# Three units' lone scores beside their state additions, one scan behind q's products, later output parts ahead of masks

## The chip, the cores and the metric

The kernel runs on one core of one Trainium2 chip. The metric is the device time of one launch in microseconds, as the median of several runs. Times in rows count from the start of the profiled span. TensorE does the matmuls, VectorE, ScalarE and GpSimd the elementwise work, SyncE issues the DMA loads and stores.

## The reference

A gated linear attention with a state of 48 x 48 for each of 8 heads and 4 sequences of 768 tokens, and behind it a gated layer of 384 to 1536 to 384 features over all 3072 tokens.

```
state = alpha[:, :, t, :, None] * state + einsum('bhd,bhe->bhde', k[:, :, t], v[:, :, t])
y[:, :, t] = einsum('bhd,bhde->bhe', q[:, :, t], state)
...
gate = 1.0 / (1.0 + exp(-(x @ w_gate)))
val = x @ w_val
out = gate * val @ w_out        # x is y with the heads side by side, [3072, 384]
```

## The kernel before

The 3072 tokens are cut into 6 groups of 512. The attention of a group is done for 4 pairs of heads, one pair at a time: a unit is one pair in one group, so there are 24 units, u = 4 g + p. Units 0 to 5 work on chunks of 128 tokens (`unit`), units 6 to 23 on chunks of 64 (`late`). The gated layer of a group takes 12 steps, one for each 128 of the 1536 hidden features; step s has f = s % 12 and group s // 12. The attention of a group runs during the steps of the group before it.

A step (`step`, L734) is two products of nine matmuls of 128x512 each (gate and value, L317: three chunks of x, by high and low parts), the sigmoid on ScalarE (L752), the gating product on VectorE (L754, in place in the PSUM bank of the value), its high part on ScalarE (hh, L756) and the remainder on VectorE (hl, L757, which reads the same bank), and the output part: six matmuls with hh and three with hl (L765), a step later. The products of a step and the outputs of units share three PSUM banks in turn, pg, pv and at2.

A late unit loads its rows of decay and k into `in0` or `in1` (L634, alternately), q into A (L640), v (L642) and a second copy of v (L645). VectorE scans the decays twice (G, L480, from `in`; F, L484), with small operations between (L482, L486, L483); GpSimd multiplies k by G in place in `in` (L488); VectorE multiplies q by F (A, two halves, L650) and transposes k (kn, 16 pieces, L663). TensorE computes the scores (L672, 16 matmuls into at0 and at1, from A and `in`), the additions to the state (L679, from kn and v, other columns of at0 and at1) and, for the unit before, the outputs (L715). VectorE then updates the state (L698, 8 operations) and multiplies the scores by a mask (L685, 4 operations); GpSimd makes vs from the state (L703). The output is split into high part (yt, L524 on ScalarE) and remainder (yt, L525 on VectorE), and two or six transfers (L532) turn it into x, of which the products of the next group read. The load into `in0` or `in1` must wait for the scores, the transposes and GpSimd of the unit that used it last.

All this is recorded as 1500 odd parts, each with an engine, a time and a key (`Plan.add`). `Plan.order` works out a due time for each part from its key and its users, and a list schedule by these ranks. Then a table of pairs, `MOVES`, is applied in order: (n, m) takes part n out of its engine's queue and puts it right behind part m. Each engine works through its own queue in that order; between engines semaphores hold. The keys of a unit are set in `begin`: o is the step at whose end the unit's output is due, y = o - 3; the state updates have y + 0.55, the masks y + 0.6, the outputs o + 0.52. The parts of `finish` (both yt and the transfers) have the key t["y"], which is None, so that only their users' due times rank them.

Of the kernel before, what the change touches and what calls it, by code (L numbers as in the profile page):

```python
# [19 lines left out]
B, H, S, D = 4, 8, 768, 48  # L20
# [36 lines left out]
def in_turns(t):  # L57
# [56 lines left out]
)  # L114


# [204 lines left out]
def chunked(ctx, tc, rows, vc, vh, weights_in, out, const, ident, flags, weights, within):  # L321
# [65 lines left out]
    mask = {n: sb.tile([P, n], F32, name=f"mask{n}") for n in (C, E)}  # L387
# [149 lines left out]
    def unit(u, g, p, t):  # L537
# [33 lines left out]
        plan.add("tensor", (0.25 * nch + 0.1, 0.5), t["A"], scores, [(inn, "k"), (inn, "q")], [x[0] for x in pas])  # L571
        plan.add("tensor", (0.09 * nch + 0.1, 0.5), t["Y"], adds, [*((knn, a) for a in range(4)), (vn, "v")], [pkn])

# [56 lines left out]
    def late(u, g, p, t):  # L630
# [50 lines left out]

        plan.add("tensor", (0.045 * EH, 0.5), t["Y"], adds, [*((knn, a) for a in range(4)), (vn, "v")], [x[0] for x in pas], fixed=True)
        for j, (pan, pa) in enumerate(pas):
# [110 lines left out]
    def begin(u):  # L794
        g, p = divmod(u, NP)
        if u < EARLY:
            t = dict.fromkeys(("load", "G", "dec", "kt", "q", "X", "kn", "Y", "A", "mask", "S", "sd", "out", "y"))
            t.update(flag=14.0 + u, run=1, e_k="vector" if u in (0,) else "gpsimd", e_q="vector" if u in (0,) else "gpsimd")
        else:
            o = last_step(u)  # L800
            y = o - 3
            t = dict(load=y - 5, G=y - 2.9, dec=y - 2, kt=y - 2.7, flag=y + 1 + 0.5 * p, q=y - 2.0, X=y - 0.50, A=y + 0.50, kn=y - 1,
                     Y=y + 0.51, mask=y + 0.6, S=y + 0.55, sd=y + 0.7, out=o + 0.52, y=None)
        return unit(u, g, p, t) if u < EARLY else late(u, g, p, t)

    def last_step(u):

        return NF * (u // NP - 1) + 10 - 3 * (NP - 1 - u % NP)

    for u in range(NP):  # L810
        for _ in begin(u):
            pass
    for f in range(NF):
        weight_piece(f, None)
    now = begin(NP)
    next(now), next(now)
    finished = {last_step(u): u for u in range(NP, NG * NP)}
    for s in range(NG * NF):
        step(s)
        if s in finished:  # L820
            u = finished[s]
            following = begin(u + 1) if u + 1 < NG * NP else iter((None, None))
            next(following)
            next(now, None)
            next(following)
            now = following
# [12 lines left out]
        out=within, in0=total[1][0:1, 0:1], scalar1=G_BOUND, scalar2=None, op0=ALU.is_le), [total[0]])  # L839
# [127 lines left out]
```

## Time and profile before

| | |
|---|---|
| three runs, us | 518.01, 518.13, 518.69; median 518.13 |
| the profiled execution, us | 518.39, span 516.6, mean granted TensorE clock 0.998 |
| TensorE (PE) | 506.4 us, 98% of the span, 4114 matmuls |
| VectorE (DVE) | 397.4 us, 77% |
| ScalarE (ACT), GpSimd (POOL) | 164.0 us, 32%; 88.6 us, 17% |
| DMA | 55.69 MB, mean 108 GB/s |

A timeline row is: start in us, length in us, engine, line, operation, what it writes <- what it reads, count, and in brackets the engine's idle time before it and what ended it. Rows that follow each other on one engine with the same line and tiles are merged. Lengths of matmuls overlap, since ends are modelled; starts are what counts. Group 2 begins with the product that starts at 196.32, group 3 at 276.89, group 4 at 357.47.

### The profile page before, as it was taken

Reading aid. Unit: us, or ns where it says so; the run is one execution under the profiler, and the core shown is the slowest. Engines: PE = TensorE matmul, PEld = TensorE weight load, DVE = VectorE, ACT = ScalarE, POOL = GpSimd, SP = SyncE. Lnnn points to the kernel's source line nnn. Section 1 sums busy time; section 2 is a strip of 40 time slices with the busy share of each in tenths; the row PEclk is TensorE's granted clock in tenths of the full one; section 3 lists DMA queues with packets and bytes.
Section 4 is the critical chain, followed back from the end, with each engine's and each line's share of the span. In section 5 each row is a group of like instructions: output and inputs, shape, how many; then the busy total and the mean of one; then the engine's idle time right before and its main releaser. Section 6 shows DMA issues by size and latency. Waiting matters only on the chain.

```text
span 516.6 us, 10389 instructions
## 1 busy us (share of the span) xinstructions
PE 506.4 (98%) x4114; PEld 422.1 (82%) x4114; DVE 397.4 (77%) x866; ACT 164.0 (32%) x304; POOL 88.6 (17%) x129
## 2 busy tenths in 40 slices
PE   7999999999999999999999999999999999999995
PEld 4688888888888888888888888887888888888884
DVE  8999999998989999979889969799978532222221
ACT  2566666624112222212222321222322212311211
POOL 4632131103121122211121201211401000000000
PEclk9999999999999999999999999999999999999999
DMA  8757796840633433421423423404522011100001
GB/s 318 289 180 233 245 282 184 242 96 32 186 81 87 121 101 130 86 93 36 128 76 93 136 41 98 115 16 126 155 34 72 3 34 36 61 1 0 1 0 65
DMA packets 23093, 55.69 MB, mean 108 GB/s; under 512 B 3712, under 2 KB 10880, under 8 KB 23040
## 3 DMA queue, kind: packets, MB, share of 16 engines
q1 hardware_dynamic: 22752, 54.58, 35.8%
q8 instruction: 34, 0.56, 0.5%
q10 hardware_dynamic: 288, 0.39, 0.2%
q14 instruction: 19, 0.16, 0.1%
HBM read 41.39 MB, written 4.72 MB: 89 GB/s over the span
## 4 chain that ended last, share of the span: by engine, by line
PE 88%; DVE 7%; DMA 2%; issue 1%; POOL 1%; ACT 0%; SPq 0%; DVEq 0%
PE po L765 26%; PE pv L317 19%; PE pg L317 18%; PE at L317 15%; PE at L672 2%; PE pg L715 1%; PE at L679 1%; DMA A<-in_rows_dram 1%; PE pv L715 1%; DVE G L480 1%; DMA x<-yt 1%; DVE kn L663 1%; PE at L715 1%; DVE F L484 1%; PE at L500 1%
## 5 line engine op out<-in xcount | busy, mean ns | idle before, releaser
L765 PE MATMUL po<-hh,w 128*128 128x512 f32 x432 | 112.8, 387 | 0.0
L317 PE MATMUL pv<-x,w 128*128 128x512 f32 x468 | 111.9, 382 | 0.0
L317 PE MATMUL pg<-x,w 128*128 128x512 f32 x459 | 109.7, 382 | 0.0
L317 PEld LDWEIGHTS pv<-x,w 128*128 128x128 f32 x468 | 87.6, 188 | 15.3
L317 PEld LDWEIGHTS pg<-x,w 128*128 128x128 f32 x459 | 85.9, 188 | 15.0 <-ACT w L452 0.2
L765 PEld LDWEIGHTS po<-hh,w 128*128 128x128 f32 x432 | 79.6, 188 | 14.2
L317 PE MATMUL at<-x,w 128*128 128x512 f32 x369 | 88.2, 382 | 0.8 <-DMA x<-yt 0.8
L317 PEld LDWEIGHTS at<-x,w 128*128 128x128 f32 x369 | 69.0, 188 | 13.1 <-issue 1.2
L663 DVE STREAM_TRANSPOSE kn<-in 32x128 f32<-32x128 f32 x224 | 67.8, 303 | 4.6 <-PE at L679 0.8
L765 PE MATMUL po<-hl,w 128*128 128x512 f32 x216 | 62.9, 383 | 0.0
L703 POOL TENSOR_TENSOR vs<-st,dec 64x384 f32<-64x384 f32 x36 | 30.6, 850 | 154.4 <-DVE st L698 153.1
L488 POOL TENSOR_TENSOR in<-in,G 128x512 f32<-128x512 f32 x21 | 28.1, 1337 | 144.2 <-DVE G L480 57.8
L765 PEld LDWEIGHTS po<-hl,w 128*128 128x128 f32 x216 | 40.4, 188 | 7.4 <-DVE hl L757 0.2
L698 DVE SCALAR_TENSOR_TENSOR st<-st,dec,at 128x48 f32<-128x48 f32 x144 | 38.0, 264 | 7.4 <-PE at L679 1.5
L754 DVE TENSOR_TENSOR pv<-pv,sg 128x512 f32<-128x512 f32 x31 | 21.2, 685 | 24.5 <-PE pv L317 22.9
L754 DVE TENSOR_TENSOR at<-at,sg 128x512 f32<-128x512 f32 x21 | 14.4, 685 | 28.6 <-PE at L317 28.6
L756 ACT CAST hh<-pv 128x512 fp32r<-128x512 f32 x31 | 18.2, 587 | 54.8 <-DVE pv L754 50.9
L752 ACT ACTIVATE sg<-pg 128x512 f32<-128x512 f32 x31 | 18.5, 597 | 47.2 <-PE pg L317 47.2
L754 DVE TENSOR_TENSOR pg<-pg,sg 128x512 f32<-128x512 f32 x20 | 13.7, 686 | 24.1 <-PE pg L317 24.0
L685 DVE TENSOR_TENSOR A<-at,mask 64x256 f32<-64x256 f32 x72 | 30.4, 422 | 1.3
L650 DVE TENSOR_TENSOR A<-A,F 64x512 f32<-64x512 f32 x36 | 25.8, 717 | 3.4 <-DMA A<-in_rows_dram 2.6
L756 ACT CAST hh<-at 128x512 fp32r<-128x512 f32 x21 | 12.3, 586 | 50.7 <-DVE at L754 50.7
(163 smaller groups left out, 511.2 us busy)
## 6 DMA issues: line engine op xcount, KB each, us to landing
in<-in_rows_dram SPq DMA_DIRECT2D x18, 516.5 KB, 3.9
raw<-in_w_dram SPq DMA_DIRECT2D x12, 575.8 KB, 4.8
x<-yt SPq DMA_DIRECT2D x30, 216.0 KB, 3.6
first_w<-in_w_dram SPq DMA_DIRECT2D x10, 575.8 KB, 5.0
A<-in_rows_dram SPq DMA_DIRECT2D x36, 128.0 KB, 3.8
v<-in_vc_dram SPq DMA_DIRECT2D x22, 192.0 KB, 4.7
vs<-in_vh_dram SPq DMA_DIRECT2D x36, 96.0 KB, 3.6
out_dram<-raw SPq DMA_DIRECT2D x10, 256.0 KB, 2.2
```

What stands on the lines that cost most here:

```text
L317: nc.tensor.matmul(out=dst, lhsT=lhs(a, i), rhs=rhs(b, i), start=(n == 0 and i == 0), stop=(n == len(todo) - 1 and i == NK - 1))
L488: plan.add(e, vec(n) if e == "vector" else pool_(n), t["kt"], lambda: getattr(nc, e).tensor_tensor(out=kT, in0=kT, in1=G, op=ALU.mult), [g ...
L650: plan.add("vector", vec(T), t["q"], lambda j=j: nc.vector.tensor_tensor(out=A[own[j], j], in0=A[own[j], j], in1=F[own[j]], op=ALU.mult), ...
L663: nc.vector.transpose(out=kn[32 * b:32 * b + 32, :, 32 * a:32 * a + 32], in_=blocks[32 * a:32 * a + 32, b])
L685: plan.add("vector", 0.42, t["mask"], lambda pa=pa, j=j, i=i: nc.vector.tensor_tensor(out=A[other[j], j].rearrange("p (c i t) -> p i c t", ...
L698: nc.vector.scalar_tensor_tensor(out=st[:, c + 1, :], in0=st[:, c, :], scalar=dec[:, c:c + 1], in1=pas[c % 2][1][:, T // 2 + c // 2 * D:T ...
L703: plan.add("gpsimd", pool_(EH * D), t["sd"], lambda j=j: nc.gpsimd.tensor_tensor(out=vs[own[j], j], in0=st[own[j], 0:EH], in1=dec[own[j]]. ...
L715: nc.tensor.matmul(out=py[R * j:R * j + D, cs], lhsT=vs[r, j, c, :], rhs=A[r, j, cs], start=True, stop=True)
L752: plan.add("scalar", act(T), None, lambda: nc.scalar.activation(out=sg, in_=got["g"][1][:, 0:T], func=AF.Sigmoid), [got["g"][0]], [sgn], s ...
L754: plan.add("vector", vec(T), None, lambda: nc.vector.tensor_tensor(out=pv, in0=pv, in1=sg, op=ALU.mult), [sgn], [pvn], soon=soon)
L756: plan.add("scalar", act(T), None, lambda: nc.scalar.copy(out=stored(hh), in_=quarters(pv)), [pvn], [hhn], soon=soon)
L765: nc.tensor.matmul(out=pso_now[m][1][:, 0:T], lhsT=weights.part("o", b, f)[:, m * P:(m + 1) * P], rhs=in_turns(h[a]), start=(f == 0 and i ...
```

## The change

```
@@ MOVES
     (664, 608), (778, 664), (663, 778), (851, 661), (736, 848), (735, 736), (606, 781), (779, 782),
+    (854, 790), (945, 914), (1239, 1208), (1539, 1508),
 )
@@ begin
             t = dict(load=y - 5, G=y - 2.9, dec=y - 2, kt=y - 2.7, flag=y + 1 + 0.5 * p, q=y - 2.0, X=y - 0.50, A=y + 0.50, kn=y - 1,
-                     Y=y + 0.51, mask=y + 0.6, S=y + 0.55, sd=y + 0.7, out=o + 0.52, y=None)
+                     Y=y + 0.51, mask=y + 0.6, S=y + 0.55, sd=y + 0.7, out=o + 0.52, y=o + 0.54 if u >= 12 else None)
```

Part 854 is the scan G of unit 8, part 790 the second half of unit 7's A*F: the scan, which stood directly ahead of the two halves in VectorE's queue, stands directly behind them. Parts 945, 1239 and 1539 are the scores of units 9, 13 and 17, parts 914, 1208 and 1508 the second products of the second steps of groups 2, 3 and 4. The new key gives the yt parts and the transfers of units 12 to 23 a rank just ahead of the next unit's state updates and masks. The added line in `MOVES` makes every line number below it one higher in the changed kernel.

TensorE's queue at the start of group 2 (w0 and w1 are the weights of its first two steps, x0 its tokens, w10 and w11 the last of group 1), before, and then changed; of the 16 rows of scores and the 8 of additions the first stand:

```order
L765 MATMUL po2_130<-hl0_121,w10_1081 128x512
L672 MATMUL at0_123<-A1_91,in1_80 64x64
...
L317 MATMUL pg0_126<-x0_115,w0_346 128x512 x9
L317 MATMUL pv0_127<-x0_115,w0_346 128x512 x9
...
L317 MATMUL at2_125<-x0_115,w1_461 128x512 x9
L317 MATMUL pg0_126<-x0_115,w1_461 128x512 x9
L679 MATMUL at0_123<-v1_82,kn0_88 48x48 x2
```

```order
L766 MATMUL po2_130<-hl0_121,w10_1081 128x512
L318 MATMUL pg0_126<-x0_115,w0_346 128x512 x9
L318 MATMUL pv0_127<-x0_115,w0_346 128x512 x9
...
L318 MATMUL at2_125<-x0_115,w1_461 128x512 x9
L318 MATMUL pg0_126<-x0_115,w1_461 128x512 x9
L673 MATMUL at0_123<-A1_91,in1_80 64x64
...
L680 MATMUL at0_123<-v1_82,kn0_88 48x48 x2
```

The scores of unit 9, which read in1, move behind two steps' products and stand directly ahead of the additions; groups 3 and 4 begin in the same way.

VectorE's queue at the same place, from the remainder of step 24 on (G1 with in1 and dec3 is unit 11, st1 unit 9), before, and then changed; of the 8 rows of state updates and the 4 of masks the first stand:

```order
L757 TENSOR_TENSOR hl0_121<-pv0_127,hh0_119 128x4x128
L782 COPY raw0_83<-po1_129 128x512
L480 SCALAR_TENSOR_TENSOR G1_95<-in1_80,d1g64_106 128x512
...
L754 TENSOR_TENSOR pg0_126<-pg0_126,sg0_117 128x512
L698 SCALAR_TENSOR_TENSOR st1_112<-st1_112,dec1_101,at0_123 128x48
...
L757 TENSOR_TENSOR hl1_122<-pg0_126,hh1_120 128x4x128
L685 TENSOR_TENSOR A1_91<-at0_123,mask64_108 64x4x64
...
L525 TENSOR_TENSOR yt0_89<-pv0_127,yt0_89 128x4x128
```

```order
L758 TENSOR_TENSOR hl0_121<-pv0_127,hh0_119 128x4x128
L783 COPY raw0_83<-po1_129 128x512
L481 SCALAR_TENSOR_TENSOR G1_95<-in1_80,d1g64_106 128x512
...
L755 TENSOR_TENSOR pg0_126<-pg0_126,sg0_117 128x512
L699 SCALAR_TENSOR_TENSOR st1_112<-st1_112,dec1_101,at0_123 128x48
...
L758 TENSOR_TENSOR hl1_122<-pg0_126,hh1_120 128x4x128
L526 TENSOR_TENSOR yt0_89<-pv0_127,yt0_89 128x4x128
L686 TENSOR_TENSOR A1_91<-at0_123,mask64_108 64x4x64
```

Only yt moves, ahead of the four masks; the scan G1 stays ahead of the gating product, the state updates and hl1. SyncE's queue is unchanged here, with the load of in1 ahead of the stores of group 1.

VectorE's queue at the start of group 3 (G1 with dec3 is now unit 15), before, and then changed:

```order
L480 SCALAR_TENSOR_TENSOR G0_94<-in0_79,d1g64_106 128x512
...
L757 TENSOR_TENSOR hl0_121<-at2_125,hh0_119 128x4x128
L782 COPY raw0_83<-po1_129 128x512
L480 SCALAR_TENSOR_TENSOR G1_95<-in1_80,d1g64_106 128x512
...
L663 STREAM_TRANSPOSE kn0_88<-in0_79 32x4x32 x8
L484 SCALAR_TENSOR_TENSOR F1_97<-in1_80,d1f_104 128x512
```

```order
L481 SCALAR_TENSOR_TENSOR G0_94<-in0_79,d1g64_106 128x512
...
L783 COPY raw0_83<-po1_129 128x512
L758 TENSOR_TENSOR hl0_121<-at2_125,hh0_119 128x4x128
...
L664 STREAM_TRANSPOSE kn0_88<-in0_79 32x4x32 x8
L481 SCALAR_TENSOR_TENSOR G1_95<-in1_80,d1g64_106 128x512
...
L485 SCALAR_TENSOR_TENSOR F1_97<-in1_80,d1f_104 128x512
```

The scan G1 moves behind the transposes of unit 14, to the place of its F1, and the load of in1 moves behind the stores of group 2 on SyncE; the start of group 4 is rearranged in the same way. On GpSimd the product of k follows its scan.

## Rows read from the trace of the kernel before

**Rows 1.** The page's first part: busy us (share of the span) x instructions.

```profile
PE 506.4 (98%) x4114; PEld 422.1 (82%) x4114; DVE 397.4 (77%) x866; ACT 164.0 (32%) x304; POOL 88.6 (17%) x129
```

**Rows 2.** Timeline of TensorE, a joined block in group 2 and what follows it.

```profile
226.00 0.69 PE L672 MATMUL at<-A,in 48*64 48x64 f32 x32
...
228.01 1.60 PE L765 MATMUL po<-hh,w 128*128 128x512 f32 x6
```

**Rows 3.** Timeline of TensorE, start of group 2: around lone scores, then additions and outputs.

```profile
194.94 0.83 PE L765 MATMUL po<-hl,w 128*128 128x512 f32 x3
...
196.32 2.26 PE L317 MATMUL pg<-x,w 128*128 128x512 f32 x9
198.41 2.14 PE L317 MATMUL pv<-x,w 128*128 128x512 f32 x9
...
206.43 0.57 PE L679 MATMUL at<-v,kn 64*48 64x48 f32 x32
...
207.97 1.60 PE L765 MATMUL po<-hh,w 128*128 128x512 f32 x6
209.40 0.82 PE L765 MATMUL po<-hl,w 128*128 128x512 f32 x3
210.06 2.14 PE L317 MATMUL at<-x,w 128*128 128x512 f32 x9
212.04 2.14 PE L317 MATMUL pg<-x,w 128*128 128x512 f32 x9
```

**Rows 4.** Timeline of VectorE and of TensorE near 165, and a later pair A*F.

```profile
161.74 1.23 DVE L480 TENSOR_TENSOR_SCAN G<-in,d1g 128x512 f32<-128x512 f32 x1
163.00 2.38 DVE L650 TENSOR_TENSOR A<-A,F 64x512 f32<-64x512 f32 x2
...
173.47 1.39 DVE L650 TENSOR_TENSOR A<-A,F 64x512 f32<-64x512 f32 x2
...
164.57 0.61 PE L765 MATMUL po<-hl,w 128*128 128x512 f32 x2
165.48 0.69 PE L672 MATMUL at<-A,in 48*64 48x64 f32 x32 [0.30 <-POOL starts L489]
```

**Rows 5.** Timeline of TensorE and of VectorE, start of group 4.

```profile
357.47 0.72 PE L317 MATMUL at<-x,w 128*128 128x512 f32 x2
...
360.60 2.14 PE L317 MATMUL pg<-x,w 128*128 128x512 f32 x9
...
351.18 1.73 DVE L685 TENSOR_TENSOR A<-at,mask 64x256 f32<-64x256 f32 x4
352.94 0.69 DVE L525 TENSOR_TENSOR yt<-at,yt 128x512 fp32r<-128x512 f32 x1
```

**Rows 6.** SyncE's waits (us, times, longest), one load's issue, line L634's landings.

```profile
SPq L634 <- PE at L672: 47.8, 9, 6.4
...
226.80 0.35 SPq L634 DMA_DIRECT2D in<-in_rows_dram  x1
...
DMA to landing us min/median/max: 3.3/3.9/6.9
```

**Rows 7.** Line L532 between 190 and 200 us: the transfers of x to group 2.

```profile
L532 SPq DMA_DIRECT2D x<-yt x2: 541/566/591, 192.2 to 192.8; - x2
...
DMA to landing us min/median/max: 3.3/3.5/3.7
```

**Rows 8.** Timeline of VectorE, start of group 2.

```profile
204.78 1.21 DVE L480 TENSOR_TENSOR_SCAN G<-in,d1g 128x512 f32<-128x512 f32 x1
...
206.61 0.70 DVE L754 TENSOR_TENSOR pg<-pg,sg 128x512 f32<-128x512 f32 x1 [0.18 <-PE pg L317]
...
209.55 0.69 DVE L757 TENSOR_TENSOR hl<-pg,hh 128x512 fp32r<-128x512 f32 x1
```

**Rows 9.** Busy time by stretch, end of the span: PE, PEld, DVE, ACT, POOL, PEclk, DMA.

```profile
511.30:514.40 3.10, 0.00 (x0) 0.00 (x0) 0.00 (x0) 0.56 (x2) 0.00 (x0) 1.00 0.73 259
514.50:516.60 2.10, 0.00 (x0) 0.00 (x0) 0.00 (x0) 0.00 (x0) 0.00 (x0) 0.50 0.00 0
```

More of the change, by code (lines that the diff above doesn't have):

```diff
@@ L802, in begin @@
             t = dict(load=y - 5, G=y - 2.9, dec=y - 2, kt=y - 2.7, flag=y + 1 + 0.5 * p, q=y - 2.0, X=y - 0.50, A=y + 0.50, kn=y - 1,
-                     Y=y + 0.51, mask=y + 0.6, S=y + 0.55, sd=y + 0.7, out=o + 0.52, y=None)
+                     Y=y + 0.51, mask=y + 0.6, S=y + 0.55, sd=y + 0.7, out=o + 0.52, y=o + 0.54 if u >= 12 else None)
         return unit(u, g, p, t) if u < EARLY else late(u, g, p, t)
```

1 row of the table MOVES is left out of this document.

## The prediction

> **What bounds the kernel now.** I read the page's engine table first: TensorE is busy for 506.4 of 516.6 us [rows 1], so a change can only shorten TensorE's own stream or a hole in it. Then I read TensorE's timeline from group 1 on, from start to start and not by busy time, since the ends are modelled. Regular work is regular to 0.02 us: a product of nine matmuls takes 1.98 us (210.06 to 212.04), three matmuls of an output part 0.66 us (209.40 to 210.06) [rows 3]. After 161 us, where the change begins, only five places depart from that, and the change goes at all five: a short wait at 165, three blocks of scores that stand alone, one ahead of the first product of each of groups 2, 3 and 4 (the first and the last of these products start at 196.32 and 357.47 [rows 3, 5]), and a wait for x at the start of group 4 [rows 5]. Last I asked what each move holds back: the queue of loads (SyncE), VectorE behind it, and the PSUM bank that TensorE writes next.
>
> **The change part by part.**
>
> *Scores joined to the state additions, three times.* A lone block puts 1.38 us between the starts of the output part before it and the product after it (194.94 to 196.32) in place of 0.66, and that product takes 2.09 in place of 1.98 (to 198.41): 0.83 us [rows 3]. Where scores, additions and outputs already stand together they take 2.01 us (226.00 to 228.01) [rows 2]; additions and outputs without scores take 1.54 (206.43 to 207.97) [rows 3]. So scores cost 0.47 us when joined: a gain of 0.36, three times, **-1.1 us**. No work is removed; one change between large and small matmuls, there and back, is.
>
> *The scan behind q's products.* Unit 8's scan G is passed by unit 7's two products A*F. Today the scan starts at 161.74, and the products, at 163.00, take 2.38 us for two where an undisturbed pair takes 1.39 [rows 4]: the scan releases GpSimd's product of k, which runs beside them. They end at 165.38, and unit 7's scores start at 165.48 [rows 4]; the profile puts the wait on GpSimd, but A is what came last. Without it the scores would start 0.44 us (two matmuls) and some 0.1 for the change of shape after 164.57, at 165.11: **-0.37 us**. Moved up, the products end at 161.74 + 1.39 = 163.13 and the wait is gone; the scan ends 1.4 us later, which hides behind the next work: its product of k is wanted only by unit 8's scores, three steps on.
>
> *Output parts ahead.* For units 12 to 23, VectorE takes the remainder yt before the four masks. At the start of group 4 a product runs from 357.47 to the next one's start at 360.60, 3.13 us where 2.09 is normal after small matmuls [rows 5]: a hole of 1.04, which the profile ends by the landing of x. The masks start at 351.18 and yt at 352.94 [rows 5], so yt and both its transfers come 1.76 us earlier. TensorE also asks 0.83 earlier, because the lone block is gone; 1.76 - 0.83 = 0.93 of 1.04 is covered. **-0.95 us**; ends -0.5 (a landing as late as the slower rows of [rows 6]) and -1.04. The masks lie on nobody's path: their reader is the unit's output three steps later. In the same edit, at the starts of groups 3 and 4, the second scan (G of the unit that reuses in1) moves behind the transposes, and the load of in1 behind the stores. Both are late enough to be harmless: today the scan F alone stands at that place with VectorE idle behind it.
>
> *What is asked earlier at group 2.* Unit 11 keeps its old rank, so x lands there as before: transfers issued at 192.2 and 192.8, landings after 3.3 to 3.7 us [rows 7], the last at 195.9 to 196.5. TensorE's third matmul now wants it at 195.60 + 0.44 = 196.04 and no longer at 196.9; the 0.37 of 165 us shifts both alike. **+0.35 us**, ends 0 and 0.6.
>
> *What the later scores hold back at group 2.* This is the term that decides. The lone scores of unit 9 read in1, and the next load into in1 (unit 11) waits for them, as the queue's own waits show at this line nine times [rows 6]. The joined block starts at 206.43 - 0.83 = 205.60, ten us later than the lone scores. In the joined pattern the load goes out 0.80 us after the block's start (226.00 to 226.80) [rows 2, 6] and lands after 3.9 us (median of 18; 3.3 to 6.9) [rows 6]: at 210.3. At this one start of a group the order of VectorE is unchanged: the scan G of unit 11 stands ahead of step 25's gating product, the state updates and the remainder hl. Today it starts at 204.78, and from there to the end of hl (209.55 + 0.69), without the 0.18 that VectorE waited at 206.61, are 5.28 us [rows 8]. Now the scan waits for the load, and behind it, in VectorE's queue, stands that whole chain: hl ends at 210.3 + 5.28 = 215.58, and 0.1 for the signal. TensorE waits for exactly that, because the second product of step 26 writes bank pg, from which hl reads. Today the product starts at 212.04, 5.61 after its block [rows 3]; joined, it would be wanted 0.47 later in its block, 6.08 after 205.60, at 211.68. The hole is 215.7 - 211.7 = 4.0 us; with 0.1 from landing to start, **+4.1 us**. It moves one for one with the landing: 3.5 at 3.3 us, 7.1 at 6.9. What is late next (the cast and remainder of step 26, some 5 us behind on VectorE) is wanted only after the hole, and costs nothing more. At groups 3 and 4 the same load is just as late, but there the scan has moved far down VectorE's queue, behind the transposes, so the hole comes once.
>
> *The clock in that hole.* No hole of 4 us with work behind it is in this trace. [...] I take 0 in the sum, the rest is a rival.
>
> **Sum**, against the profiled execution's own 518.39 us: -1.1 - 0.37 - 0.95 + 0.35 + 4.1 = +2.0, that is **520.4 us**. The profiled execution lies 0.26 us above the median of the three runs (518.13) and within their range; I leave that in, as the landing is as likely late as early.
>
> **The rivals.**
>
> *The hole also costs the clock.* [...] For it: [rows 9]. Against it: there the idle time was endless, here the load may land early. Price: the 2.1 us that the trace shows at the lower level, without a return, would cost 1.05; one whole product costs 1.98. That gives 521.4 to 522.4. [...]
>
> *Faster: the load doesn't hold the scan.* If in1 came in time, by a reload that need not wait for the scores, or by slack in bank pg that I have overlooked, all other terms stand: 518.39 - 1.1 - 0.37 - 0.95 + 0.35 = 516.3. It decides below a hole of 0.8 us (516.3 + 0.8 = 517.1, 0.2% under the median before). Against it speak the nine waits of [rows 6] and the order of VectorE; for it only that the other two starts of a group are clean.
>
> *A smaller hole, no change.* If the landing takes 3.3 us, x at group 2 is in time, and group 4 gives its full 1.04, the sum is -1.1 - 0.37 - 1.04 + 3.5 = +1.0: 519.4; with part of the chain quicker than in the row, because GpSimd's product of k no longer runs beside it, 518.5 to 519.2.
>
> *The output parts don't help.* If the transfers of x are late for their own reasons (landings reach 6.9 in [rows 6]), the 0.95 falls away: 521.3, within the range of the forecast and the clock rival.
>
> **How the numbers follow.** Forecast (hole of 3.5 to 4.7, clock kept) 0.42, its own range 519.4 to 521.3; the clock rival 0.32; a smaller hole or none of consequence 0.15; no hole 0.11. About 0.2%, 1.04 us, is what a measurement of this kernel can tell from no change: 517.1 to 519.2. So faster 0.11, same 0.15, slower 0.74. The range 518.6 to 522.4 leaves out the no-hole case, a part of the small hole below, and landings over 5 us with a fallen clock above.
>
> **What would show it.** In the changed kernel's timeline: (1) three joined blocks of some 2.0 us at the starts of groups 2, 3 and 4, and no scores between two products of 128x512; (2) no wait of scores near 165 us, with the pair A*F at 1.4 us; (3) the third matmul of group 4 without a wait for x; (4) at about 206 us a SyncE wait of some 6 us for the scores, VectorE idle some 5 us ahead of the scan G with a landing of in as what ended it, and TensorE idle some 4 us ahead of the second product of step 26, ended by hl; (5) the granted clock after that hole, 0.50 or 1.00. I am wrong if (4) is missing, or if the scan waits but TensorE doesn't: then bank pg isn't what binds, and the time falls to 516 to 517.

## The result, and the profile after

The changed kernel takes **522.96 us** (median of 6 runs, 522.69 to 523.72); the kernel before took 518.15 beside it (517.86 to 518.69). The ratio is 1.0095, 95% interval 1.0082 to 1.0108: slower by about 4.8 us. The execution that was profiled is the slowest of the six, 523.72 us with a span of 521.9; against the profiled execution before (518.39) that is +5.33 us, and the readings below account for this difference. Line numbers of the changed kernel are one higher; the experiments have those of before.

One correction to the names on record, which touches no time: units were numbered four too low in the moves and scans. The moved scores are those of units 13, 17 and 21; the scan that waits at the start of group 2 is unit 15's; the scan near 162 us is unit 12's and the products A*F there unit 11's; at group 3 they are units 19 (G1) and 18 (transposes). That unit 11 keeps its old rank is right as it stands.

The page's first part (busy us, share of the span, instructions) and its row of the granted clock in 40 slices:

```profile
PE 508.2 (97%) x4114; PEld 424.0 (81%) x4114; DVE 399.2 (76%) x866; ACT 163.9 (31%) x304; POOL 86.7 (17%) x129
...
PEclk9999999999999999799999999999999999999999
```

TensorE's busy time rose by 1.8 us against [rows 1], with the same instructions: some of them ran slower, and the clock's row has one slice of 13 us at 0.7. The rest of the loss is idle time. Where both lie stands in TensorE's timeline (start, duration, what it does, in brackets the idle time ahead of it and what ended it):

```profile
164.68 0.61 PE L766 MATMUL po<-hl,w 128*128 128x512 f32 x2
165.21 0.70 PE L673 MATMUL at<-A,in 48*64 48x64 f32 x32
...
195.34 0.61 PE L318 MATMUL pg<-x,w 128*128 128x512 f32 x2
196.27 1.80 PE L318 MATMUL pg<-x,w 128*128 128x512 f32 x7 [0.33 <-DMA x<-yt]
197.91 2.14 PE L318 MATMUL pv<-x,w 128*128 128x512 f32 x9
...
205.93 0.69 PE L673 MATMUL at<-A,in 48*64 48x64 f32 x32
...
207.94 1.61 PE L766 MATMUL po<-hh,w 128*128 128x512 f32 x6
...
210.05 2.15 PE L318 MATMUL at<-x,w 128*128 128x512 f32 x9
216.79 4.21 PE L318 MATMUL pg<-x,w 128*128 128x512 f32 x9 [4.59 <-DVE hl L758]
220.79 1.85 PE L766 MATMUL po<-hh,w 128*128 128x512 f32 x6
222.48 0.82 PE L766 MATMUL po<-hl,w 128*128 128x512 f32 x3
...
363.62 2.14 PE L318 MATMUL at<-x,w 128*128 128x512 f32 x9
365.61 2.14 PE L318 MATMUL pg<-x,w 128*128 128x512 f32 x9
367.58 1.48 PE L766 MATMUL po<-hh,w 128*128 128x512 f32 x6
```

Read from start to start, as [rows 3] were:

- Near 165 us the scores follow the output part after 0.53 us; in [rows 4] it was 0.91. Gain 0.38.
- The joined block of group 2 takes 2.01 us (205.93 to 207.94), as in [rows 2]. Groups 3 and 4 have the same block with the same 2.01 and 2.02. Gain 3 x 0.36 = 1.08.
- At group 4 the products follow each other after 1.99 and 1.97 us; the hole of 1.04 of [rows 5] is gone. Gain 1.04.
- At group 2 the first product runs for 2.57 us in place of 1.98 and waits inside for x. Cost 0.59.
- Behind the first product of step 26 (210.05 + 1.98 = 212.03) TensorE stands until 216.79, ended by hl. Cost 4.76: the hole.
- The product out of that hole takes 4.00 us in place of 1.98, the output part behind it 1.69 in place of 1.32. Cost 2.39.

The sum is -0.38 - 1.08 - 1.04 + 0.59 + 4.76 + 2.39 = **+5.24**, of 5.33 measured. The chain behind the hole begins on SyncE and goes on in VectorE, answering to [rows 6] and [rows 8]. SyncE's timeline, the landing of that one load (min, median and max are the same issue), and VectorE's timeline:

```profile
206.72 0.33 SPq L635 DMA_DIRECT2D in<-in_rows_dram  x1
```

```profile
DMA to landing us min/median/max: 4.7/4.7/4.7
```

```profile
211.54 1.23 DVE L481 TENSOR_TENSOR_SCAN G<-in,d1g 128x512 f32<-128x512 f32 x1 [6.96 <-DMA in<-in_rows_dram]
...
213.12 0.67 DVE L755 TENSOR_TENSOR pg<-pg,sg 128x512 f32<-128x512 f32 x1
213.71 2.42 DVE L699 SCALAR_TENSOR_TENSOR st<-st,dec,at 128x48 f32<-128x48 f32 x8
216.05 0.68 DVE L758 TENSOR_TENSOR hl<-pg,hh 128x512 fp32r<-128x512 f32 x1
```

The load of in1 goes out 0.79 us after the joined block begins and lands after 4.7; VectorE has stood idle for 6.96 us ahead of the scan, and from the scan's start to the end of hl it needs 5.19. Then TensorE's product of bank pg begins.

The granted clock, by stretches (the stretch and its length, the busy time of PE, PEld, DVE, ACT and POOL, then the clock, the DMA share and GB/s):

```profile
212.00:214.00 2.00, 0.20 (x1) 0.00 (x0) 1.93 (x6) 0.17 (x1) 1.10 (x1) 1.00 0.95 279
214.00:216.00 2.00, 0.00 (x0) 0.00 (x0) 1.73 (x7) 1.41 (x3) 0.40 (x3) 0.68 0.28 80
216.00:218.00 2.00, 1.21 (x3) 1.03 (x4) 1.96 (x5) 0.00 (x0) 1.78 (x3) 0.50 0.00 0
218.00:220.00 2.00, 2.00 (x7) 1.54 (x6) 1.91 (x5) 0.00 (x0) 0.00 (x0) 0.50 0.67 99
220.00:222.00 2.00, 2.00 (x7) 1.64 (x6) 1.90 (x6) 0.72 (x2) 0.00 (x0) 0.62 0.75 113
222.00:225.00 3.00, 3.00 (x15) 2.55 (x15) 2.85 (x8) 0.59 (x1) 0.00 (x0) 1.00 0.03 6
```

It falls to 0.50 within the hole, and TensorE works at that level from 216.79 until between 220 and 222 us.

### The profile page after: what moved, and what is told of

Read it like the earlier page. It is cut to its first block, busy times and chain, and to the rows that moved or that the text cites. A ratio compares the mean times of both kernels' runs of the same rounds, so it can differ in the third digit from the quotient of the medians.

```text
span 521.9 us, 10390 instructions
## 1 busy us (share of the span) xinstructions
PE 508.2 (97%) x4114; PEld 424.0 (81%) x4114; DVE 399.2 (76%) x866; ACT 163.9 (31%) x304; POOL 86.7 (17%) x129
## 4 chain that ended last, share of the span: by engine, by line
PE 90%; DVE 5%; DMA 2%; SPq 1%; issue 1%; POOL 0%; ACT 0%; DVEq 0%
PE po L766 27%; PE pg L318 20%; PE pv L318 19%; PE at L318 15%; PE at L673 2%; PE pg L716 1%; PE at L680 1%; DMA A<-in_rows_dram 1%; PE pv L716 1%; PE at L716 1%; DVE F L485 1%; DMA x<-yt 1%; DVE G L481 1%; PE at L501 1%; PE at L564 0%
## 5 line engine op out<-in xcount | busy, mean ns | idle before, releaser
L318 PE MATMUL pg<-x,w 128*128 128x512 f32 x459 | 111.9, 387 | 4.9 <-DVE hl L758 4.6
L318 PEld LDWEIGHTS pg<-x,w 128*128 128x128 f32 x459 | 87.0, 190 | 21.0 <-DVE hl L758 5.0
L481 DVE TENSOR_TENSOR_SCAN G<-in,d1g 128x512 f32<-128x512 f32 x22 | 26.8, 1220 | 7.4 <-DMA in<-in_rows_dram 7.0
```

Source lines behind the costliest of these rows:

```text
L318: nc.tensor.matmul(out=dst, lhsT=lhs(a, i), rhs=rhs(b, i), start=(n == 0 and i == 0), stop=(n == len(todo) - 1 and i == NK - 1))
L481: plan.add("vector", scan(n), t["G"], lambda: nc.vector.tensor_tensor_scan(out=G[:, ::-1], data0=az[:, n:0:-1], data1=d1g[size], initial=0 ...
```

## The experiments

The theory after this reading: the late load holds the scan, the scan stands ahead of hl in VectorE's queue, hl holds bank pg; and the clock is a second cost on top. The rivals: another edit makes the loss; the late load hurts by another way (the queue of loads, GpSimd); the slow product has nothing to do with the hole. Entries of the table are pairs (part, part it goes behind); each diff shows only the end of the table that changes, against the kernel that its text names or the run just ahead of it. Each time stands beside runs of the kernel before on the same chip, by which the ratio is taken.

**The first move of scores, taken out and put in alone.**

```diff
-    (854, 790), (945, 914), (1239, 1208), (1539, 1508),
+    (854, 790), (1239, 1208), (1539, 1508),
```

> The changed kernel without its first move of scores: those of the unit at group 2 stand alone again, ahead of group 2's first product; all else as changed. Theory: no hole, no fallen clock, no x asked earlier: 518.15 - 0.72 (two blocks joined) - 0.38 - 1.04 = 516.0 us. Rival (the scan behind q's products or the output parts cause the loss): 520 or more.

Measured: 516.38 us (516.31 to 516.48), ratio 0.9964 [0.9950, 0.9978]. TensorE has no wait left between 155 and 440 us. So the other two joined blocks, the scan and the output parts are worth their gain, and the loss hangs on this one entry.

> The kernel before with one move alone: the scores at the start of group 2 go to the state additions. Theory: the whole loss is in this one move: 518.2 - 0.36 + 0.5 (x) + 4.76 (hole) + 1.7 (clock) = 524.8 us, between 523.5 and 525.5. Rival (the loss needs the other edits too, the other order of masks and yt above all): 518 to 520.

(Its edit: the kernel before with the entry (945, 914) and nothing else.) Measured: 526.07 us (524.92 to 526.55), ratio 1.0146 [1.0133, 1.0159]. TensorE's waits in that kernel (us, times, longest), and its timeline behind the hole:

```profile
PE pg L317 <- DVE hl L757: 4.7, 1, 4.7
```

```profile
217.30 4.21 PE L317 MATMUL pg<-x,w 128*128 128x512 f32 x9 [4.65 <-DVE hl L757]
221.30 2.42 PE L765 MATMUL po<-hh,w 128*128 128x512 f32 x6
223.56 0.82 PE L765 MATMUL po<-hl,w 128*128 128x512 f32 x3
```

The hole is there without any other edit, as long as in the changed kernel. The time is 0.6 above the range expected: behind the hole the product takes 4.00 and the output part 2.26 us, 2.96 more than at full clock, where 1.7 was put down. The clock's price is not one number.

**The scan at two more places.** If the scan's place ahead of hl decides, all three joined blocks must fail alike in the kernel before, whose VectorE keeps the scan there at groups 2, 3 and 4.

```diff
-    (606, 781), (779, 782),
+    (606, 781), (779, 782), (945, 914), (1239, 1208), (1539, 1508),
```

> The kernel before with all three moves of scores and nothing else, so that VectorE and the queue of loads keep their order and the second scan stands ahead of hl at groups 2, 3 and 4. Theory (it is the place of that scan that decides): three holes of 4.7 us with a fallen clock behind each, 526.1 + 2 x (4.7 + 1.7 - 0.36) + 0.8 (x at group 4) = 539 us, between 535 and 541. Rival (only the start of group 2 is special, by its queue of stores and loads): 525 to 526.

Measured: 539.35 us (538.42 to 539.66), ratio 1.0407 [1.0393, 1.0421]. The waits of TensorE, at groups 4, 2 and 3:

```profile
PE at L317 <- DVE hl L757: 5.9, 1, 5.9
PE pg L317 <- DVE hl L757: 4.5, 1, 4.5
PE pv L317 <- DVE hl L757: 3.4, 1, 3.4
```

The loads of in1 that belong to them, at groups 4, 2 and 3, one issue each:

```profile
DMA to landing us min/median/max: 6.1/6.1/6.1
...
DMA to landing us min/median/max: 4.7/4.7/4.7
...
DMA to landing us min/median/max: 3.5/3.5/3.5
```

Three holes, a slow product behind each (4.00, 3.75 and 4.01 us in place of 1.98, at groups 4, 2 and 3), and each wait is 0.1 to 0.2 us shorter than its landing: 2.6 us more landing between the shortest and the longest, 2.5 us more hole. The hole does move one for one with the landing.

**The scan out of the way.** The four VectorE operations from that scan on go behind the transposes of unit 14, all else stays.

```diff
-    (1539, 1508),
+    (1539, 1508), (1077, 1019), (1078, 1077), (1081, 1078), (1079, 1081),
```

> The changed kernel, with one thing moved on VectorE alone: the second scan G at the start of group 2, with the three small operations behind it, goes behind the transposes of the unit before, where it stands at groups 3 and 4. TensorE's order, the later scores and the late load of in1 stay. Theory (the scan that waits for the load holds back hl, and with it TensorE): hole and fallen clock are gone, 518.15 - 1.1 - 0.38 - 1.04 + 0.59 = 516.2 us; TensorE goes from the first to the second product of step 26 in 1.98 us. Rival (the late load itself hurts, by the queue of loads or by GpSimd's product of k behind the scan): a hole of 2 us or more stays somewhere between 206 and 235 us, time 518.5 or more.

Measured: 520.96 us (519.97 to 521.69), ratio 1.0048 [1.0035, 1.0062]. The hole behind step 26's first product is gone, as expected, but the rival was right on the time. TensorE's and VectorE's timelines:

```profile
212.06 2.14 PE L317 MATMUL pg<-x,w 128*128 128x512 f32 x9
...
220.77 1.60 PE L765 MATMUL po<-hh,w 128*128 128x512 f32 x6 [0.62 <-ACT hh L756]
...
227.49 0.54 PE L679 MATMUL at<-v,kn 64*48 64x48 f32 x32
230.47 2.04 PE L715 MATMUL at<-A,vs 128*48 128x64 f32 x32 [2.44 <-POOL st L694]
232.44 2.34 PE L765 MATMUL po<-hh,w 128*128 128x512 f32 x6
234.62 0.82 PE L765 MATMUL po<-hl,w 128*128 128x512 f32 x3
```

```profile
216.68 1.40 DVE L650 TENSOR_TENSOR A<-A,F 64x512 f32<-64x512 f32 x2 [4.25 <-DMA A<-in_rows_dram]
...
229.68 0.69 DVE L757 TENSOR_TENSOR hl<-at,hh 128x512 fp32r<-128x512 f32 x1 [0.65 <-ACT hh L756]
```

VectorE, no longer held by in1, waits 4.25 us for A instead, whose loads stand behind that of in1 in SyncE's queue: they go out at 209.5 and 210.6 us and land after 6.7 to 7.2, in the kernel before at 208.1 and 208.7, landing after 2.9 to 3.2. Between the two stand the three stores of group 1, which the waiting load holds back as well: they go out from 207.18 us, in the kernel before from 203.19. Two new waits of TensorE follow, of 0.62 and 2.44 us, and behind the longer one the block's outputs take 1.97 us in place of 1.03 and the output part 2.18 in place of 1.43: the clock again, granted at 0.52 from 230.50 to 232.50 us. The profile puts the wait of 2.44 down to GpSimd. The next run took that at its word; its edit is against the run just shown.

```diff
-    (1079, 1081),
+    (1079, 1081), (1082, 963), (1083, 1082),
```

> As the run in which only the second scan of group 2 was moved behind the transposes, and in addition GpSimd takes the two products vs of the unit before ahead of the product of k that needs this scan. Theory (three queues stand behind the late load: VectorE by the scan, GpSimd by the product of k, the loads of A by the queue of loads): of the waits that were left there the one of 2.44 us for GpSimd goes, and with it the fallen clock behind it; the wait of 0.6 us for hh, by the late A, stays: 518.2 - 1.1 - 0.38 - 1.04 + 0.42 (x) + 0.62 = 516.7 us. Rival (GpSimd is late for another reason): 520.5 to 521.

Measured: 522.05 us (520.40 to 523.55), ratio 1.0081 [1.0065, 1.0098]. This theory fell. The timelines of GpSimd, TensorE and VectorE:

```profile
209.44 1.73 POOL L703 TENSOR_TENSOR vs<-st,dec 64x384 f32<-64x384 f32 x2 [5.78 <-DVE st L698]
```

```profile
230.56 2.04 PE L715 MATMUL at<-A,vs 128*48 128x64 f32 x32 [2.51 <-issue]
```

```profile
216.61 1.49 DVE L650 TENSOR_TENSOR A<-A,F 64x512 f32<-64x512 f32 x2 [4.07 <-DMA A<-in_rows_dram]
...
224.72 1.22 DVE L480 TENSOR_TENSOR_SCAN G<-in,d1g 128x512 f32<-128x512 f32 x1
...
226.43 2.10 DVE L484 TENSOR_TENSOR_SCAN F<-in,d1f 128x512 f32<-128x512 f32 x1
...
229.77 0.69 DVE L757 TENSOR_TENSOR hl<-at,hh 128x512 fp32r<-128x512 f32 x1 [0.65 <-ACT hh L756]
```

GpSimd now has vs ready at 211.2, and TensorE waits until 230.56 all the same. Those products write bank at2, from which hl of step 27's first product reads, and that hl ends at 230.46. It is late because VectorE stood 4.07 us for A, and also because the moved scan, its small operations and the scan F now run ahead of it on VectorE, from 224.72 to 228.53; in the kernel before only F (1.23 us) stands there. The edit that took the scan out of one hl's way put it into the way of another. So the later scores delay three things through one load: the scan behind it on VectorE, the loads of A behind it on SyncE, and, through either, the remainder hl whose bank TensorE needs next.

**Everything in the order of groups 3 and 4.** The load of in1 goes behind the three stores, which are ready long before it, and yt of unit 11 ahead of its masks; then, in a second kernel, the scan F behind hl as well.

```diff
-    (1083, 1082),
+    (1083, 1082), (1071, 898), (876, 841),
```

> The changed kernel with everything at the start of group 2 in the order of groups 3 and 4: the second scan behind the transposes, GpSimd's products vs ahead of the product of k, the load of in1 behind the three stores, and the remainder yt of unit 11 ahead of its masks. Theory: no wait of TensorE is left between 160 and 420 us, and the three joined blocks give their full gain: 0.36 less than the 516.38 of the run with the first scores lone, 516.0 us; A lands before 214. Rival (A or x stays late): 516.5 or more.

Measured: 516.46 us (515.87 to 516.77), ratio 0.9966 [0.9953, 0.9979]. One wait of TensorE is left, 0.57 us ahead of the same outputs:

```profile
PE at L715 <- issue: 0.6, 1, 0.6
```

```diff
-    (876, 841),
+    (876, 841), (1080, 981),
```

> As the run with everything at group 2 in the order of groups 3 and 4, and in addition the scan F there goes behind the remainder hl of step 27's first product, as it stands at group 3. Theory (the 0.57 us for which the output products of the next block wait are for that hl, since they write the bank it reads, and not for GpSimd): the wait goes, 516.46 - 0.57 = 515.9 us. Rival (that block waits for GpSimd's vs): 516.5.

Measured: **516.00 us** (515.82 to 516.00), ratio 0.9960 [0.9946, 0.9973], with no wait of TensorE between 155 and 440 us. The bank was the cause of that last wait. A is still not early: asked for at 207.5 and 208.1, it lands after

```profile
DMA to landing us min/median/max: 5.3/5.4/5.5
```

where the kernel before, with nothing of in1 ahead of it, had 2.9 to 3.2 at the same place; VectorE waits 1.00 us for it, and TensorE no longer waits for VectorE. With the load of in1 ahead of it in the queue, A lands some 2.3 us later, after 5.4 against 3.1 us (medians); no run here tells a wait in the queue from a load that only shares the transfer rate.

This version beats the kernel before. Whether it beats the one with the first scores left alone (516.38) stays open: the two intervals overlap.

**x at group 2.** The kernel with only the scan moved, and yt of unit 11 ahead of its masks.

```diff
-    (1079, 1081),
+    (1079, 1081), (876, 841),
```

> As the run in which only the second scan of group 2 was moved behind the transposes, and in addition the remainder yt of unit 11 goes ahead of that unit's four masks, as the units from 12 on have it. Theory: x for group 2 lands 1.7 us earlier, the wait of 0.59 us for it goes: 516.2 - 0.59 = 515.6 us. Rival (x there is late by its transfers, not by yt): 516.2.

Measured: 521.03 us (520.72 to 521.33), ratio 1.0054 [1.0040, 1.0067]. The wait for x is gone (the product goes from 195.34 to 197.32 in 1.98 us), so yt was what made x late; the waits behind A are those of the run without it, 0.47 and 2.43 us. The profiled execution is 0.66 us below that run's (521.03 against 521.69), the medians are alike (521.03 against 520.96): whether the gain reaches the end stays open.

**The clock by itself.** Behind step 26's first product, where the hole is:

```diff
+                products(nc, ...); [nc.tensor.matmul(out=pso[0][1][:, 0:T], lhsT=wz, rhs=wz..., start=False, stop=False) for _ in range(21 if s == 26 and nm == "g" else 0)]
```

(The three dots stand for the call that makes the product, which stays as it was, and for the operand's repetition to 512 columns.)

> The changed kernel with 21 added matmuls of zeros (128x512, adding nothing) behind the first product of step 26, where TensorE stands idle for 4.8 us: they take some 4.5 us and are there to keep TensorE's clock up, so the hole stays and only the clock can differ. Theory (hole and clock are two costs): the second product of step 26 starts where it did, ended by hl, with the granted clock at 1.00, and takes 1.98 us in place of 4.0: 1.0 to 2.4 us less than the changed kernel, 520.5 to 521.9. Rival (the slow product has another cause, or the clock costs nothing on the whole): 522.7 to 523.5.

The added operand is made of the identity's halves and is not all zeros as stated, so one bank of the output gets something added; the time is read for the clock alone. Measured: 521.28 us (520.67 to 521.61), ratio 1.0057 [1.0043, 1.0070]. TensorE's timeline:

```profile
212.11 4.71 PE L745 MATMUL po<-ident 128*128 128x512 bf16 x21
216.86 2.26 PE L317 MATMUL pg<-x,w 128*128 128x512 f32 x9
218.96 1.48 PE L765 MATMUL po<-hh,w 128*128 128x512 f32 x6
```

And its granted clock there:

```profile
216.00:218.00 2.00, 1.95 (x9) 1.20 (x8) 1.96 (x5) 0.00 (x0) 1.86 (x3) 1.00 0.00 0
```

The product starts where it did (216.86; in the changed kernel 216.79), at a granted clock of 1.00 in place of 0.50, and takes 2.10 us in place of 4.00. The ratio is 0.0038 lower than the changed kernel's, 2.0 us. The slow product was the clock, and the clock was 2.0 of the 4.8 us by which the changed kernel is slower.

**The small parts alone.** The kernel before with the new rank of the output parts and no entry:

> The kernel before with the rank of the output parts alone (units 12 to 23), no entry of the table added. The planner then puts the scores of groups 3 and 4 behind the additions by itself, so two of the three joined blocks are there without an entry. Theory: 518.2 - 0.72 - 1.04 = 516.4 us; the wait of the scores near 165 us stays. Rival (the gain hangs on the entries): 517.2.

Measured: 516.66 us (516.49 to 517.05), ratio 0.9974 [0.9965, 0.9983]; the gain is there without an entry, since with the new rank the planner itself joins the scores of groups 3 and 4 and moves the second scan behind the transposes. And the scan's entry (854, 790) alone:

> The kernel before with the scan G behind q's two products, near 162 us, and nothing else. Theory: the scores there start 0.37 us earlier, 518.1 - 0.37 = 517.8 us. Rival (the stream of TensorE gives it back later, or the moved scan makes something else late): 518.1.

Measured: 517.76 us (517.50 to 518.18), ratio 0.9993 [0.9984, 1.0002]. The size is the one expected, but the interval holds 1. In its trace the scores come 0.53 us after the output part, as in the changed kernel; whether those 0.3 us reach the end is not settled by the times.

## Why the prediction was right or wrong

The direction and the place were right. 522.96 us lies 0.56 above the range and 2.6 above the time named. Point by point:

- **What bounds the kernel.** Right: every change of the time is a change in TensorE's own stream or a hole in it.
- **Joined scores, -1.1.** Right: 1.08.
- **Scan behind q's products, -0.37.** Right in the trace: 0.38.
- **Output parts ahead, -0.95.** Right in size, 1.04, the end named for it; the run with the rank alone has no wait for x either. (The other end, -0.5, and the rival of transfers as late as 6.9 us rest on [rows 6], which are landings of in; those of x are [rows 7], 3.3 to 3.7 us.) At groups 3 and 4, where scan and load move as well, TensorE has no wait, as argued.
- **x asked earlier, +0.35.** The mechanism was right (the run with yt ahead takes the wait away), the size 0.59, at the end given as 0.6. (From transfers issued at 192.2 and 192.8 and landings of 3.3 to 3.7 us, the last comes at 196.1 to 196.5, not from 195.9.)
- **The hole, +4.1.** The chain was right in every link: issue 0.79 us after the block (0.80 foreseen), scan to hl 5.19 (5.28), then bank pg. The term was short by the landing: 4.7 us, where the median of [rows 6] had been taken, 3.9. The slope of one for one, which was on record, would have given 4.9 at that landing; measured 4.76. This is the smaller of the two steps that failed: the median of 18 landings over the whole span stood for one load at one place. At this place the load went out at 206.7 to 207.2 us and landed after 4.7 us in the changed kernel, 4.6 in the run with the scan moved, 4.8 with the first scores alone moved and 4.7 with three joined blocks; in the kernel before it went out at 200.0 and landed after 3.4. So with the move its landing changed too. What lengthens it isn't shown: at groups 3 and 4 of the run with three joined blocks it landed after 3.5 and 6.1.
- **The clock in the hole, 0.** This is the larger of the two steps that failed: the sum put the clock at nothing, and the rival that had it was priced at up to 1.98 us for one whole product. No run shows the 0: behind each hole of 3.4 us or more the product took 3.75 to 4.01 us in place of 1.98. The profiled run paid 2.39, since part of the output part behind the product ran at a lowered clock as well (0.62 from 220 to 222 us), and filling the hole gave back 2.0. [Rows 9] showed the fall, from 1.00 to 0.50; the way back, which no row of before showed, took longer than one product, until after 220 us. The range's upper end was that rival's, with the landing at 3.9; a landing of 4.7 and a fallen clock together lie above it, and that is what came.
- **The rivals.** The one with the fallen clock came, over its price. That of no hole, by slack in bank pg, is ruled out by the four holes of the two kernels that move scores and nothing else.
- **What is late next.** The sentence that nothing more is late after the hole holds only under the hole: with the scan moved away, the loads of A, behind in1 on SyncE, were the next wait (0.62 us of TensorE's, by way of hh), and together with the scans G and F ahead of the next hl they gave one of 2.44 us, behind which the clock fell again, to 0.52. The queue of loads was named as something to look at, but only the load of in1 itself was followed through it, not the loads of A behind it.

With the measured landing and 2.0 for the clock, the sum on record, +2.0, would have been 2.0 + 0.8 + 2.0 = +4.8, and the difference of the medians is 4.81. That it fits so closely is partly luck: x cost 0.24 more than foreseen, while the hole came 0.14 under its own slope and the output parts gave 0.09 more, and the profiled execution, in which the landing was read, paid 2.39 for the clock and not 2.0.

## What to carry to other kernels

A consumer that is moved later to sit better on its own engine also moves the reload of the buffer it reads; follow that reload through every queue it stands in (the engine that waits for it first, then the transfers behind it), until each has been asked what is late next. Where a forecast has a hole in TensorE's stream with work behind it, put the clock into the sum, not beside it: here the work behind holes of 3.4 to 5.9 us took 1.8 to 3.0 us longer. And a releaser named by the profile for a wait on several semaphores is a candidate: here GpSimd was named, and it was a remainder on VectorE that still held the bank.

## What the runs showed of the hardware

The price of the fallen clock is not ordered by the idle time before it. In the kernel with three holes, waits of 4.5, 3.4 and 5.9 us were followed by 1.8, 3.0 and 2.4 us of slower work. The rows behind the shortest of them:

```profile
303.00:305.00 2.00, 1.66 (x4) 1.37 (x5) 1.93 (x5) 0.00 (x0) 1.34 (x3) 0.50 0.00 0
305.00:307.00 2.00, 2.00 (x6) 1.52 (x6) 1.94 (x4) 0.00 (x0) 0.00 (x0) 0.50 0.01 2
307.00:309.00 2.00, 2.00 (x6) 1.57 (x5) 1.90 (x7) 0.74 (x3) 0.00 (x0) 0.50 0.83 125
309.00:311.00 2.00, 2.00 (x10) 1.66 (x9) 1.90 (x6) 0.57 (x1) 0.00 (x0) 0.92 0.61 99
```

From 303.34, where it takes up work, TensorE is busy throughout, and the granted clock is still 0.50 up to 309 us, 5.7 us later. In the run with the scan moved, the clock fell after a wait of 2.44 us: the granted clock was 1.00 up to 230.40 and 0.52 in the stretch from 230.50 to 232.50. Behind the one wait of 0.57 us, in the run with everything in the order of groups 3 and 4, the work kept its pace: the output part that follows took 1.45 us (228.26 to 229.71), as the one at 207.47 to 208.92 with no wait before it. What sets the length in the single case, these runs don't tell.
